# Streamed tiles and weights at many distances modulo 512 bytes

## Chip, cores and metric

One core of one Trainium2 chip runs the whole program. The metric is device time in microseconds, the median of three runs. The four inputs of attention and the weights of two feed-forward stages lie in HBM; the result goes back to HBM.

## What is computed

The reference has three stages, one behind the other, in float32 (some inputs arrive as 64-bit words, which the kernel turns into float32 itself):

```python
state = gamma * state + k_t v_t^T ; y_t = scale * q_t state     # 4 batches, 8 heads, 768 steps, 64 wide
xn = x / rms(x) * rms_g                                          # x: 3072 tokens x 512
x  = (silu(xn @ w_gate) * (xn @ w_val)) @ w_out                  # 512 -> 1536 -> 512
h  = x @ w_in ; solu = h * softmax(h) ; out = layernorm(solu) * g_ln @ w_out2   # 512 -> 1024 -> 512
```

## The kernel before

The 3072 tokens go in six blocks of 512 (`NB`), numbered 0 to 5. A block's hidden width of 1536 goes in twelve groups of 128 (`NM`). Every large product is made of three matmuls: each float32 operand is split into a high and a low part (type fp32r), and `mm3` (lines 775 to 778) adds high by high, high by low and low by high into one PSUM bank. A matmul has two operands in SBUF: the weights (`lhsT`, 128 columns, 512 bytes per partition), which a weight-load instruction brings into TensorE, and the streamed tile (`rhs`, mostly 512 columns, 2048 bytes per partition), which runs past them.

Per group `m`, `bc_block` (line 813) streams the normalised activations `xnh` and `xnl` past the gate and val weights (tiles `w`, tag `w4`, four buffers) into the banks GB and VB (`gv`), makes silu(gate) times val and its two parts `ah` and `al` (tag `r2`, eight buffers), and one group later streams these past the output weights (tag `wo`, two buffers) into four banks X0 to X3 (`cmm`, line 800). From block 1 on, these weights are loaded from a scratch copy in HBM by `w_load` (line 699), on the queue of SyncE. In block 0 the even groups use the same tiles and the odd ones the tile `CV`. Block 5 forms the gate and val products from sums of quarters (`seven_block`, matmuls on line 888, 256 streamed columns); there the four summed activations stand in tiles of the tags `rq`, `rk`, `kd` and `qd`. The last stage of a block streams `w2ih` and `w2il` past parts of x (`d_mm`, or the quarter products on line 1150, which also stream `xnh`, `xnl` and tiles of `w4` past tiles of `r2` and `x2`), transposes the result (line 1018) and streams `w2oh` and `w2ol` past the transposed parts, which are `r2` tiles (`e_mm`, line 1036). Attention of the next block is woven between these matmuls.

Addresses. The program keeps a row of fixed tiles (pool `cp`), and behind them the rotating tiles (pool `wp`), tag by tag in the order of the first request, all buffers of a tag one behind the other, each rounded up to 32 bytes per partition. `spacer` and `gap` reserve bytes that nothing uses. Nearly every tile is 2048 or 4096 bytes long, so a tag's buffers all have the same remainder of their address modulo 512. "Distance" below is the address of the streamed tile minus that of the weights loaded while it streams (those of the next matmul), modulo 512. Slices of a tile start at multiples of 512 bytes, so a distance depends on the tiles alone. The remainders of the kernel before:

| tiles | remainder |
|---|---|
| w2ih, w2il, xnh, xnl, U, w2oh, w2ol, CV, x2, r2, f4, st, w4, wo, rv, A | 448 |
| rq, rk, kd, qd | 352 |

So every product of fp32r parts has distance 0, but for the four summed tiles of block 5, which have 416.

Of the kernel before, what the change touches and what calls it, by code (L numbers as in the profile page):

```python
# [18 lines left out]
P = 128  # L19
# [23 lines left out]
def retention_moe_kernel(ctx: ExitStack, tc: tile.TileContext, qk0, q2, kt, kv, wpk, w2i, w2o,  # L43
# [3 lines left out]
    wp = ctx.enter_context(tc.tile_pool(name="wp", bufs=1))  # L47
# [13 lines left out]
    def spacer(n, name):  # L61
        cp.tile([P, n // 4], F32, tag=name, name=name)

    spacer(320, "sp0")
    QK = cp.tile([P, NCB, 2, 4, P], F32, tag="w2ih", name="QK")
    KV = cp.tile([P, NCB, 2, 512], F32, tag="w2il", name="KV")
    w2 = {}
# [8 lines left out]

    cnt = [0]

    def wt(tag, shape, dt, bufs):
        cnt[0] += 1  # L80
        return wp.tile(shape, dt, tag=tag, name=f"{tag}_{cnt[0]}", bufs=bufs)

    gaps = set()

    def gap(name, n):
        if name not in gaps:
            gaps.add(name)
            wp.tile([P, n // 4], F32, tag=name, name=name, bufs=1)

    def st():  # L90
        return wt("st", [P, 512], F32, 3)

    def f4():
        return wt("f4", [P, 2, 512], F32, 3)

    def r2():
        return wt("r2", [P, 512], F32R, 8)
# [36 lines left out]
            nc.vector.tensor_tensor(out=new, in0=new, in1=sv, op=ALU.add)  # L134

    def unit_load(gc, u):
        gap("gq", 416)
        tq = wt("rq", [P, 4, P], F32, 2)
        nc.sync.dma_start(tq, q2[gc, u])
        if u == 0:  # L140
            rawk[gc] = wt("rk", [P, 4, P], F32, 2)
            nc.sync.dma_start(rawk[gc], kt[gc])
        gap("gr", 96)
        tv = wt("rv", [P, 512], F32, 2)
        nc.sync.dma_start(tv, kv[gc, u])
        raw[gc, u] = (tq, tv)
# [701 lines left out]
    bufs = {"w4": 4, "rv": 2, "x2": 4}  # L848
# [513 lines left out]
    for i in (m0, m1, m2, m3) if SCOPE else (m1, m2, m3):  # L1362
        after.enter_context(tc.issue_after(i.ins))
    pk(3), first_decay(3), state(3), upd(3)
    unit_load(NCB, 0)
    unit_load(NCB, 1)
    unit_prep(NCB, 0)

# [116 lines left out]
```

## Time and profile before

| | |
|---|---|
| median of three runs | 980.13 us (978.42 to 980.45) |
| span of the profiled execution | 977.1 us |
| TensorE busy in it | 964.0 us, 5868 matmuls |
| VectorE, GpSimd, ScalarE busy | 504.5, 435.2, 423.0 us |
| weight loads on TensorE | 802.8 us, beside the matmuls |

The profiled execution has its span, from the first instruction to the last, as its own time; the median of the runs is 3.0 us longer (980.13 less 977.1), which holds what lies around the span. Matmuls overlap in the profile: the time that one costs is the spacing from its start to the next one's, and its listed duration is longer by a fixed part.

### The profile page before, as it was taken

What the parts mean: (1) busy time and instruction counts of PE and PEld (TensorE: products, weight loads), DVE (VectorE), ACT (ScalarE), POOL (GpSimd) and SP (SyncE); (2) the same over time, 40 slices, a digit from 0 to 9 for tenths busy, and PEclk for the clock granted to TensorE, in tenths of its full rate; (3) what the DMA queues carried; (4) which work ended last, traced back from release to release, by engine and by line L of the source; (5) the groups of instructions that cost most, each with busy time, mean ns of one, the idle gap of its engine ahead of it and who ended that gap; (6) DMA issues with size and microseconds to landing.
All of it is one profiled execution on the core that took longest, in us unless ns stands there. A gap on an engine that the chain in (4) does not pass through costs nothing.

```text
span 977.1 us, 15991 instructions
## 1 busy us (share of the span) xinstructions
PE 964.0 (99%) x5868; PEld 802.8 (82%) x5868; DVE 504.5 (52%) x996; ACT 423.0 (43%) x824; POOL 435.2 (45%) x473
## 2 busy tenths in 40 slices
PE   8999999999999999999999999999999999999998
PEld 7878787888888888888888888888888888999987
DVE  5788784662465743433574233476233366343473
ACT  4767664582345444222355122346312246321254
POOL 6976873671142494443437234438132426300022
PEclk9799999999999999999999999999999999999999
DMA  9799999887513116898833789952698954798501
GB/s 347 246 329 404 351 318 386 316 322 231 189 35 96 56 44 198 294 309 271 290 115 117 277 292 352 311 171 80 204 340 297 322 187 132 242 319 293 192 1 44
DMA packets 94990, 227.64 MB, mean 233 GB/s; under 512 B 10816, under 2 KB 36800, under 8 KB 93888
## 3 DMA queue, kind: packets, MB, share of 16 engines
q1 hardware_dynamic: 86128, 201.44, 60.3%
q10 hardware_dynamic: 8784, 25.17, 6.7%
q8 instruction: 47, 0.77, 0.3%
q14 instruction: 31, 0.25, 0.1%
HBM read 184.63 MB, written 41.94 MB: 232 GB/s over the span
## 4 chain that ended last, share of the span: by engine, by line
PE 90%; POOL 3%; DMA 2%; DVE 2%; ACT 2%; issue 1%; SPq 0%; ACTq 0%; POOLq 0%
PE X L776 11%; PE X L778 10%; PE X L777 10%; PE GB L776 7%; PE GB L778 6%; PE GB L777 6%; PE VB L776 6%; PE VB L778 6%; PE VB L777 6%; PE SB L119 3%; PE X L1150 3%; PE GB L1150 2%; PE VB L1150 2%; PE YB L119 2%; PE VB L888 2%; PE YB L888 2%
## 5 line engine op out<-in xcount | busy, mean ns | idle before, releaser
L795 DVE TENSOR_TENSOR f<-VB,f 128x512 f32<-128x512 f32 x60 | 41.4, 690 | 131.3 <-PE VB L778 117.4
L777 PE MATMUL X<-r,wo 128*128 128x512 f32 x260 | 101.7, 391 | 0.0
L778 PE MATMUL X<-r,wo 128*128 128x512 f32 x260 | 101.4, 390 | 0.0
L776 PE MATMUL X<-r,wo 128*128 128x512 f32 x260 | 99.9, 395 | 0.0
L824 ACT ACTIVATE f<-GB 128x512 f32<-128x512 f32 x60 | 35.7, 595 | 142.7 <-PE GB L778 141.9
L100 ACT CAST r<-f 128x512 fp32r<-128x512 f32 x72 | 44.5, 619 | 117.2 <-DVE f L795 99.0
L677 POOL TENSOR_TENSOR st<-st,x 128x512 int32<-128x512 int32 x52 | 70.5, 1359 | 46.5 <-DVE st L676 11.8
L776 PE MATMUL GB<-xnh,w 128*128 128x512 f32 (+1 forms) x220 | 86.5, 393 | 1.1 <-ACT xnh L100 0.8
L777 PE MATMUL GB<-xnl,w 128*128 128x512 f32 (+1 forms) x220 | 85.7, 390 | 0.2 <-DVE xnl L101 0.2
L776 PE MATMUL VB<-xnh,w 128*128 128x512 f32 (+1 forms) x220 | 85.7, 390 | 0.0
L778 PE MATMUL GB<-xnh,w 128*128 128x512 f32 (+1 forms) x220 | 85.5, 389 | 0.1
L778 PE MATMUL VB<-xnh,w 128*128 128x512 f32 (+1 forms) x220 | 85.2, 387 | 0.3 <-POOL w L101 0.3
L777 PE MATMUL VB<-xnl,w 128*128 128x512 f32 (+1 forms) x220 | 85.1, 387 | 0.0
L101 DVE TENSOR_TENSOR r<-f,r 128x512 fp32r<-128x512 f32 x72 | 60.5, 842 | 32.5 <-ACT r L100 32.0
L572 POOL TENSOR_TENSOR x<-x 128x512 f32<-128x512 f32 x24 | 31.5, 1314 | 97.4 <-DMA x<-scr 73.7
L101 POOL TENSOR_TENSOR r<-st,r 128x512 fp32r<-128x512 f32 x8 | 10.9, 1367 | 114.7 <-ACT r L100 114.7
L241 POOL TENSOR_TENSOR qd<-rq,qtab_t 128x512 f32<-128x512 f32 x14 | 18.8, 1343 | 92.2 <-DMA rq<-in_q 74.5
L776 PE MATMUL X<-w2oh,r 128*128 128x512 f32 (+1 forms) x144 | 57.3, 398 | 1.1 <-ACT f L1058 0.6
L778 PEld LDWEIGHTS X<-r,wo 128*128 128x128 f32 x260 | 48.8, 188 | 10.2
L776 PEld LDWEIGHTS X<-r,wo 128*128 128x128 f32 x260 | 48.7, 188 | 10.2 <-ACT r L100 0.2
L777 PEld LDWEIGHTS X<-r,wo 128*128 128x128 f32 x260 | 48.8, 188 | 9.9 <-issue 0.2
L778 PE MATMUL X<-w2oh,r 128*128 128x512 f32 (+1 forms) x144 | 55.6, 386 | 0.0
(452 smaller groups left out, 2489.5 us busy)
## 6 DMA issues: line engine op xcount, KB each, us to landing
w<-scr SPq DMA_DIRECT2D x96, 512.0 KB, 4.9
wo<-scr SPq DMA_DIRECT2D x59, 512.0 KB, 5.0
x<-in_wpk SPq DMA_DIRECT2D x36, 512.0 KB, 6.7
x<-scr SPq DMA_DIRECT2D x25, 512.0 KB, 5.9
sscr<-x SPq DMA_DIRECT2D x24, 512.0 KB, 7.8
scr<-CV ACTq DMA_DIRECT2D x18, 512.0 KB, 6.6
rv<-in_kv SPq DMA_DIRECT2D x24, 256.0 KB, 4.1
scr<-w ACTq DMA_DIRECT2D x12, 512.0 KB, 6.1
```

Source lines behind the costliest of these rows:

```text
L100: h = nc.scalar.copy(hi, src)
L101: (lo_eng or nc.vector).tensor_tensor(out=lo, in0=src, in1=hi.bitcast(F32), op=ALU.subtract)
L119: return lambda: nc.tensor.matmul(out, lhsT=lhsT, rhs=rhs, start=start, stop=stop)
L572: nc.gpsimd.tensor_tensor(out=w[:, 0, :], in0=w[:, 0, :], in1=w[:, 1, :], op=ALU.add)
L677: nc.gpsimd.tensor_tensor(out=ti, in0=ti, in1=lo, op=ALU.add)
L776: nc.tensor.matmul(ps, lhsT=lh, rhs=rh, start=start, stop=False)
L777: nc.tensor.matmul(ps, lhsT=lh, rhs=rl, start=False, stop=False)
L778: return nc.tensor.matmul(ps, lhsT=ll, rhs=rh, start=False, stop=stop)
L795: recent["dve"] = nc.vector.tensor_tensor(out=a, in0=GV[1], in1=silu[:, 0, :], op=ALU.mult)
L824: recent["act"] = nc.scalar.activation(s[:, 0, :], GV[0], AF.Silu)
L888: nc.tensor.matmul(ps, lhsT=x, rhs=y[:, k, :], start=start and k + i == 0, stop=k == 1 and i == 2, skip_group_check=True)
L1150: last["mm"] = nc.tensor.matmul(bank, lhsT=x[:, k, ts_], rhs=y[:, k, :], start=start and k + i == 0, stop=k == 1 and i == 2, skip_group_ch ...
```

## The change

The spacer ahead of the fixed tiles goes (320 bytes), and one gap shrinks by 384. The 704 bytes are given to three tags: each buffer of `r2` is 16 bytes longer (32 with the rounding), of `w4` 80 (96), of `wo` 8 (32), and half of the tiles of `wo`, those with an odd running number, begin 8 bytes into their buffer. No instruction is added, removed or moved, and no size of a transfer changes.

```diff
-    spacer(320, "sp0")
...
+    pads = {"r2": 16, "w4": 80, "wo": 8}
+
     def wt(tag, shape, dt, bufs):
         cnt[0] += 1
-        return wp.tile(shape, dt, tag=tag, name=f"{tag}_{cnt[0]}", bufs=bufs)
+        n = 1
+        for x in shape[1:]:
+            n *= x
+        if tag not in pads:
+            return wp.tile(shape, dt, tag=tag, name=f"{tag}_{cnt[0]}", bufs=bufs)
+        t = wp.tile([P, n + pads[tag] // 4], dt, tag=tag, name=f"{tag}_{cnt[0]}", bufs=bufs)
+        o = 2 * (cnt[0] % 2) if tag == "wo" else 0
+        t = t[:, o:o + n]
...
     def unit_load(gc, u):
-        gap("gq", 416)
+        gap("gq", 32)
```

Worked out from these sizes, the remainders become:

| tiles | before | after |
|---|---|---|
| w2ih, w2il, xnh, xnl, U, w2oh, w2ol, CV, x2 | 448 | 128 |
| r2, buffers 0 to 7 | 448 | 128, 160, 192, 224, 256, 288, 320, 352 |
| f4, st | 448 | 384 |
| w4, buffers 0 to 3 | 448 | 384, 480, 64, 160 |
| wo, buffers 0 and 1 | 448 | 256 or 264, 288 or 296 |
| rq, rk, kd, qd | 352 | 352 |
| rv, A | 448 | 448 |

## Rows read from the trace of the kernel before

**Rows 1.** The page: span, busy time by engine, granted clock and DMA by slice.
```profile
span 977.1 us, 15991 instructions
PE 964.0 (99%) x5868; PEld 802.8 (82%) x5868; DVE 504.5 (52%) x996; ACT 423.0 (43%) x824; POOL 435.2 (45%) x473
PEclk9799999999999999999999999999999999999999
DMA  9799999887513116898833789952698954798501
```

**Rows 2.** The page: chain of waits that ended last, by engine.
```profile
PE 90%; POOL 3%; DMA 2%; DVE 2%; ACT 2%; issue 1%; SPq 0%; ACTq 0%; POOLq 0%
```

**Rows 3.** Busy time by stretch: stretch, length, busy us per engine, clock, DMA share, GB/s.
```profile
165.00:760.00 595.00, 595.00 (x3639) 487.62 (x3638) 275.99 (x560) 237.11 (x473) 260.37 (x285) 1.00 0.65 219
760.00:925.00 165.00, 164.08 (x1003) 145.35 (x1002) 78.24 (x180) 58.76 (x115) 40.99 (x48) 1.00 0.71 244
```

**Rows 4.** Timeline of TensorE behind a pause: start us, duration us, operation.
```profile
302.19 0.47 PE L776 MATMUL X<-w2oh,r 128*128 128x512 f32 x1
302.50 0.39 PE L777 MATMUL X<-w2ol,r 128*128 128x512 f32 x1
...
304.58 0.39 PE L777 MATMUL X<-w2ol,r 128*128 128x512 f32 x1
...
305.49 0.39 PE L778 MATMUL X<-w2oh,r 128*128 128x512 f32 x1
```

**Rows 5.** Timeline of TensorE's weight loads in the same stretch.
```profile
304.59 0.19 PEld L778 LDWEIGHTS X<-w2oh,r 128*128 128x128 f32 x1
```

**Rows 6.** Matmuls of line 1150: duration ns min/median/max.
```profile
L1150 PE MATMUL X<-w2ih,x x32: 389/389/389, 484.1 to 943.8; 128*128 128x512 f32 x32
L1150 PE MATMUL GB<-xnl,r x24: 389/389/389, 488.2 to 935.6; 128*128 128x512 f32 x24
```

**Rows 7.** Matmuls of line 888: duration ns min/median/max.
```profile
L888 PE MATMUL SB<-xnh,w x20: 277/283/283, 821.4 to 910.2; 128*128 128x256 f32 x20
L888 PE MATMUL SB<-rq,w x18: 277/280/283, 833.9 to 910.9; 128*128 128x256 f32 x18
L888 PE MATMUL VB<-qd,A x36: 277/280/283, 843.0 to 917.2; 128*128 128x256 f32 x36
```

**Rows 8.** Groups of TensorE by line and form: count, busy us, mean ns, idle before.
```profile
L777 PE MATMUL X<-r,wo 128*128 128x512 f32 x260 | 101.7, 391 | 0.0
L776 PE MATMUL GB<-xnh,w 128*128 128x512 f32 x212 | 83.5, 394 | 0.8 <-ACT xnh L100 0.8
L776 PE MATMUL X<-w2oh,r 128*128 128x512 f32 x136 | 55.0, 404 | 1.1 <-ACT f L1058 0.6 <-ACT r L1021 0.5
L776 PE MATMUL GB<-w2oh,r 128*128 128x512 f32 x48 | 18.9, 395 | 0.0
L1150 PE MATMUL X<-w,r 128*128 128x512 f32 x48 | 12.2, 389 | 0.0
```

**Rows 9.** Matmuls of line 776 that write X from r2 and wo: duration ns min/median/max.
```profile
L776 PE MATMUL X<-r,wo x260: 387/389/501, 49.3 to 922.9; 128*128 128x512 f32 x130
```

**Rows 10.** Transposes of line 1018: duration ns min/median/max.
```profile
L1018 PE MATMUL X<-ident,f x136: 270/272/327, 280.3 to 965.4; 128*128 128x128 f32 x136
```

**Rows 11.** DMA issues: KB each, median us from issue to landing.
```profile
wo<-scr SPq DMA_DIRECT2D x59, 512.0 KB, 5.0
```

More of the change, by code (lines that the diff above doesn't have):

```diff
@@ L77, in retention_moe_kernel @@
     cnt = [0]
+    pads = {"r2": 16, "w4": 80, "wo": 8}
     def wt(tag, shape, dt, bufs):
         cnt[0] += 1
-        return wp.tile(shape, dt, tag=tag, name=f"{tag}_{cnt[0]}", bufs=bufs)
+        n = 1
[6 more added lines that the diff above has]
+        t = t[:, o:o + n]
+        if len(shape) == 3:
+            t = t.rearrange("p (a x) -> p a x", a=shape[1])
+        if len(shape) == 4:
+            t = t.rearrange("p (a b x) -> p a b x", a=shape[1], b=shape[2])
+        return t
     gaps = set()
```

## The prediction

> **What bounds the kernel now.** I read the page first. TensorE is busy 99% of the span and every other compute engine about half of it [rows 1]. The chain of waits that ended last lies to 90% on TensorE [rows 2], and in the long middle (165 to 760 us) the engine is busy for all of the 595 us, in block 5 for 164.08 of 165 us [rows 3]. The granted clock stays at its upper level, 2.4 GHz, in both stretches [rows 3]. So the time is the sum of the spacings of TensorE's matmuls, and only what changes a spacing changes the time. In the timeline the reader is to look at starts, not at durations: four spacings from 304.58 to 305.49 us take 0.91 us, 227 ns each, where 512 columns at 2.4 GHz would be 213 ns [rows 4]. The listed duration is 389 ns there, so a spacing is the duration less 162 ns, and durations in the other views can be compared in single ns. The next matmul's weights are loaded at the same time: the load for the matmul of 304.81 starts at 304.59, 0.01 us behind the matmul of 304.58 [rows 4, 5]. So two streams read SBUF side by side, and their distance modulo 512 is what the edit alters.
>
> Two more things are to be seen. First, at distance 0 the matmul repeats itself to the ns: 32 and 24 in a group with minimum, median and maximum all 389 [rows 6]. Second, behind a pause it doesn't: the nine spacings from 302.50 to 304.58 take 2.08 us, 231.1 ns each, 4 ns more than the settled ones [rows 4]. It takes several matmuls to find the pace of 227. I read this as a repeating state that the equal spacing of equal pairs makes possible; that it needs one constant distance is my inference, no row shows it for 512 columns.
>
> **The change part by part.**
>
> The instructions. None is added, moved or removed; engines other than TensorE have the same tile sizes, and their remainders stay multiples of 32 bytes, but for half of the output weights. I cost ScalarE, VectorE and GpSimd at nothing: they are idle about half of the span, TensorE covers them, and if that cover went, one of their operations late by tens of ns would be lost in spacings of the same size.
>
> How many matmuls get another distance. Gate and val: six groups of 212 (two banks, three matmuls), 1272. Output products: three of 260, 780. Last products: three of 136 and three of 48, 552. Quarter products with an r2 or w4 tile: 48, and by the same view 144 more, 192 [rows 8]. Sum 2796. A few keep distance 0 (r2's buffer 0 against the fixed tiles, some pairs at the seams of two groups); by the remainders about 2650 change. Gate and val get 256, 160, 64 and 480, one value for the twelve matmuls of a tile. The output products get 18 values that differ between neighbours, since the high and low parts lie in different buffers. The last products get 480 down to 288 in steps of 32, again different between neighbours.
>
> What another distance costs. For 512 columns no row has one, so I bound it. The nearest rows are those of 256 columns in block 5: at distance 0 the median is 283 ns, at 416 it is 280, and the extremes are 277 and 283 on both sides [rows 7]. So the low end is -3 ns per matmul, 2650 x -3 ns = -8.0 us; with the minimum (-6 ns) -15.9 us. On the other side stands the stretch in which 512 columns have not settled: +4 ns, 2650 x 4 ns = +10.6 us. The upper end of the sum I take as twice that, +8 ns, +21 us, should a worse pace repeat. I take the unsettled stretch as the value, because it is the row with the same column count and the same tiles, but only where the distance changes from matmul to matmul: output, last and quarter products, 1524 less some 150 that keep distance 0, 1374 x 4 ns = +5.5 us. Gate and val have a constant distance for twelve matmuls, so I let them settle there, and count a fresh start for each of 1272 / 12 = 106 tiles; a start costs up to 9 x 4 = 36 ns [rows 4], half of that taken, since some starts will fall near the pace: 106 x 18 ns = +1.9 us.
>
> Block 5 itself. Its products on line 888 with xnh and xnl stand at 0 against w4 and rv and leave it; at -3 ns for some 180 of them -0.5 us. The summed tiles have 416 or other values before and after, taken as no change.
>
> Transposes. Lines of f4 move from distance 256 to 0. No row prices it, and the nearest is block 5's 3 ns between two distances [rows 7, 10]: 160 x 3 ns, up to 0.5 us either way, taken as +0.2.
>
> The 8 bytes. Half of the output weights start 8 bytes off. Their load lands in 5.0 us [rows 11], and a group of 36 matmuls takes 36 x 0.227 = 8.2 us, with two buffers, so a load that got slower by half would still be in time; past that it would end a wait. Cost taken: nothing. As weights, the 0.19 us load [rows 5] lies beneath a spacing of 0.227.
>
> Sum: 5.5 + 1.9 - 0.5 + 0.2 = +7.1 us. The profiled 977.1 us become 984.2; with the 3.0 us by which the median exceeds the span, 987.2.
>
> A rule that speaks against all of this: the Trainium skill, "SBUF — State Buffer", section "Who interferes with whom", gives TensorE two independent read ports, one for the streamed operand and one for the weights, and says that it never waits on anyone. By that rule a distance can't matter. Rows 7 differ by 3 ns between distances with the same columns, and the trace so far doesn't bear the rule out fully; it is rival A's ground.
>
> **The rivals.**
>
> A, nothing happens. The extra 14 ns per matmul come from the switch of weights and not from addresses. For it: spacing less columns is about the same for 512 and 256 columns at distance 0 (389 - 162 - 213 = 14; 283 - 162 - 107 = 14) [rows 6, 7]. Against it: rows 7. Time 980.1, chance 0.15.
>
> B, faster. Distance 0 is the bad one because both streams start in the same place, and every other distance gives what 416 gives in block 5: -3 ns each, -8.0 us, 972.1; with the minimum of the rows, 964. For it: the median of 280 against 283 [rows 7]. Against it: at 256 columns a weight load of 0.19 us is nearly as long as the matmul and both may wait for each other; at 512 columns it is not, and there unsettled matmuls are slower than settled ones, not faster. Decides from an average spacing under 227. Chance 0.25.
>
> C, slower still: a worse pace repeats in all 2650, +8 ns, 1001. Nothing but groups' means above 389, as 394 and 404 [rows 8], speaks for it, and these hold the matmuls at pauses. Chance 0.07.
>
> D, the output weights come late: the loads into 8-byte remainders take longer than a group (8.2 us against 5.0 [rows 11]), and TensorE waits in each of some 50 groups. From 1 us late per group +50 us. DMA is below full share in the middle (0.65 and 0.71 [rows 3]), which speaks against it. Chance 0.03.
>
> **How the numbers follow.** The forecast itself, 981.5 to 996 around 987.2, has 0.50. Slower by over 0.2% (2 us, about what a measurement of this kernel can tell from no change) is the forecast with C and D, 0.60; within 0.2% is A, 0.15; faster is B, 0.25. The range has to take in B's 972 and stop short of D and the far end of C: 971 to 1000; the forecast's own range is 981.5 to 996.
>
> **What would show it.** Right: TensorE's count stays 5868, its idle time stays near 13 us, and the listed mean durations rise, for the output products from 391 to about 395, with the median no longer the minimum plus 2 [rows 8, 9]; gate and val rise less, and their median stays at 389. Line 1150's groups with x alone stay at 389/389/389. Wrong: durations below 389 as the rule for a whole group (B), all medians at 389 as before (A), or a new wait of TensorE for wo (D).

## The result: 13.9 us slower, and the profile after

The changed kernel takes 993.54 us (median of four runs, 989.81 to 994.85) against 979.62 us of the kernel before on the same chip: ratio 1.0135, 95% interval 1.0114 to 1.0155 (the quotient of the two medians is 1.0142). That is +13.9 us, with 11.2 to 15.2 by the interval. The prediction said 987.2 us in a range of 971 to 1000: the sign is right, the size (+7.1 us in its sum) is half of what was measured.

First the page of the changed kernel, the lines that answer to [rows 1, 2].

```profile
span 991.8 us, 15991 instructions
PE 978.5 (99%) x5868; PEld 806.2 (81%) x5868; DVE 506.2 (51%) x996; ACT 422.8 (43%) x824; POOL 436.1 (44%) x473
PEclk8899999999999999999999999999999999999999
...
PE 90%; POOL 3%; DMA 3%; DVE 2%; ACT 1%; issue 1%; SPq 1%; ACTq 0%; DVEq 0%; POOLq 0%
```

The span grew by 14.7 us (991.8 less 977.1) and TensorE's busy time by 14.5 (978.5 less 964.0), with the same 5868 matmuls. Its idle time is 13.3 us after 13.1. So no wait was added, the chain is as before, and the matmuls themselves stand further apart. The table by stretch says the same (columns as in [rows 3]):

```profile
165.00:760.00 595.00, 595.00 (x3573) 480.94 (x3573) 271.23 (x551) 236.19 (x471) 261.76 (x285) 1.00 0.63 216
760.00:925.00 165.00, 164.08 (x1001) 142.86 (x1000) 79.36 (x180) 57.27 (x113) 42.19 (x49) 1.00 0.72 246
```

TensorE is busy for all of the 595 us at granted clock 1.00 and starts 66 matmuls fewer in them (3573 for 3639). Now the timeline of TensorE at the place of [rows 4], behind the same pause:

```profile
308.76 0.48 PE L789 MATMUL X<-w2oh,r 128*128 128x512 f32 x1
309.07 0.39 PE L790 MATMUL X<-w2ol,r 128*128 128x512 f32 x1
...
311.86 0.40 PE L790 MATMUL X<-w2ol,r 128*128 128x512 f32 x1
312.09 0.39 PE L791 MATMUL X<-w2oh,r 128*128 128x512 f32 x1
```

From 309.07 to 312.09 lie thirteen spacings, 232.3 ns each. In the kernel before the first nine took 231.1 ns each and the next ones 227. Here the pace of 227 is not found, as the prediction had taken it for these products. The groups by line (lines are 13 further down than before; columns as in [rows 8]):

```profile
L790 PE MATMUL X<-r,wo 128*128 128x512 f32 x260 | 102.6, 394 | 0.0
...
L789 PE MATMUL GB<-xnh,w 128*128 128x512 f32 x212 | 84.2, 397 | 0.9 <-ACT xnh L113 0.9
...
L789 PE MATMUL X<-w2oh,r 128*128 128x512 f32 x136 | 55.4, 407 | 1.0 <-ACT f L1071 0.6 <-ACT r L1034 0.5
...
L1163 PE MATMUL X<-w,r 128*128 128x512 f32 x48 | 12.5, 395 | 0.0
```

The means rise by 3 ns for the output and last products, and by 3 for gate, which the prediction had let settle; the quarter products with w4 rise by 6. The rows below give minimum, median and maximum of single groups; they answer to [rows 9, 6, 7, 10], and the second fence is gate, in the kernel before and in the changed one (it holds 8 matmuls of 256 columns beside the 212).

```profile
L789 PE MATMUL X<-r,wo x260: 387/394/506, 52.1 to 937.1; 128*128 128x512 f32 x130
```

```profile
L776 PE MATMUL GB<-xnh,w x220: 283/389/579, 34.6 to 780.2; 128*128 128x512 f32 x106, 128*128 128x256 f32 x4
...
L789 PE MATMUL GB<-xnh,w x220: 278/394/580, 36.3 to 793.5; 128*128 128x512 f32 x106, 128*128 128x256 f32 x4
```

```profile
L1163 PE MATMUL X<-w,r x48: 389/394/399, 495.7 to 957.0; 128*128 128x512 f32 x48
...
L1163 PE MATMUL X<-w2ih,x x32: 387/389/397, 493.0 to 958.4; 128*128 128x512 f32 x32
```

```profile
L901 PE MATMUL SB<-xnh,w x20: 276/280/283, 835.4 to 924.4; 128*128 128x256 f32 x20
L901 PE MATMUL SB<-rq,w x18: 274/281/287, 848.0 to 925.1; 128*128 128x256 f32 x18
```

```profile
L1031 PE MATMUL X<-ident,f x136: 270/272/328, 286.7 to 980.2; 128*128 128x128 f32 x136
```

The output products' median went from 389 to 394: it is the rule that moved, not the edge. So did gate's, where the prediction's sign was a median that stays at 389. On line 1163 the pair w2ih against x2, which keeps its distance of 0, still has the median 389, though its extremes are now 387 and 397, while its neighbour with w4 and r2 has the median 394. Of 256 columns, xnh past w fell from 283 to 280. The transposes are unchanged. The load of the output weights lands later than in [rows 11], and no wait of TensorE names it:

```profile
wo<-scr SPq DMA_DIRECT2D x59, 512.0 KB, 5.6
```

The last transpose row holds a ruler that the experiments need. From the first transpose to the last, the kernel before takes 685.1 us (965.4 less 280.3 [rows 10]) and the changed one 693.5: +8.4 us in that stretch. The other 6.3 us (14.7 less 8.4) lie before it. Nearly half of them are still the same matter, in blocks 0 and 1: if the two traces' matmuls are matched one by one in the order of their starts, the changed kernel is 3.6 us behind at 111 us and 6.4 at the first transpose (286.7 less 280.3), and from 111 to 280 us both have the granted clock at 1.00. The changed kernel and then the kernel before, in that stretch:

```profile
111.00:280.00 169.00, 167.85 (x843) 135.68 (x842) 93.59 (x142) 87.43 (x154) 86.04 (x70) 1.00 0.80 283
```

```profile
111.00:280.00 169.00, 167.98 (x874) 137.78 (x875) 95.39 (x152) 89.41 (x159) 85.84 (x71) 1.00 0.79 278
```

So 11.2 of the 14.7 us come behind 111 us, at the upper level of the clock. The 3.6 us before that lie where the granted clock still moves. The next rows are the stretch from 12 to 16 us, in the changed kernel and then in the kernel before, and one group of block 0 whose distance is 0 in both, after and then before.

```profile
12.00:16.00 4.00, 4.00 (x47) 3.55 (x45) 1.67 (x5) 1.81 (x6) 2.47 (x4) 0.58 1.03 408
```

```profile
12.00:16.00 4.00, 3.46 (x47) 3.27 (x48) 2.74 (x7) 2.26 (x7) 3.85 (x5) 1.00 1.04 404
```

```profile
L789 PE MATMUL GB<-xnh,CV 128*128 128x512 f32 x24 | 10.2, 426 | 0.0
```

```profile
L776 PE MATMUL GB<-xnh,CV 128*128 128x512 f32 x24 | 9.7, 405 | 0.0
```

The granted clock is 0.58 there, so mostly the lower level of 1.2 GHz, where the kernel before has the upper one of 2.4 GHz throughout (1.00); TensorE itself was busy for all of the 4 us, and for 8.62 of the 12 us ahead of them. From 60 to 100 us the clock is 0.96 against 1.00, and a group whose distance did not change got 21 ns dearer in the mean. The kernel before has such a stretch too, at another place: over the first 111 us its clock is 0.95, that of the changed kernel 0.92. Stretches at the lower level lie in the first 180 us of every profile of the whole kernel below, at places that differ. So a single profile is compared from the first transpose on, which leaves out what blocks 0 and 1 cost ahead of it, and whole times by their medians.

### The profile page after: what moved, and what is told of

It reads as the page before. It is cut to its first block, busy times and chain, and to the rows that moved or that the text cites. A ratio compares the mean times of both kernels' runs of the same rounds, so it can differ in the third digit from the quotient of the medians.

```text
span 991.8 us, 15991 instructions
## 1 busy us (share of the span) xinstructions
PE 978.5 (99%) x5868; PEld 806.2 (81%) x5868; DVE 506.2 (51%) x996; ACT 422.8 (43%) x824; POOL 436.1 (44%) x473
## 4 chain that ended last, share of the span: by engine, by line
PE 90%; POOL 3%; DMA 3%; DVE 2%; ACT 1%; issue 1%; SPq 1%; ACTq 0%; DVEq 0%; POOLq 0%
PE X L789 11%; PE X L791 10%; PE X L790 10%; PE GB L789 7%; PE GB L791 7%; PE GB L790 7%; PE VB L789 6%; PE VB L791 6%; PE VB L790 6%; PE X L1163 3%; PE SB L132 3%; PE GB L1163 2%; PE VB L1163 2%; PE YB L132 2%; PE VB L901 2%; PE YB L901 2%
## 5 line engine op out<-in xcount | busy, mean ns | idle before, releaser
L790 PE MATMUL X<-r,wo 128*128 128x512 f32 x260 | 102.6, 394 | 0.0
L791 PE MATMUL X<-r,wo 128*128 128x512 f32 x260 | 102.4, 394 | 0.0
L789 PE MATMUL X<-r,wo 128*128 128x512 f32 x260 | 101.1, 400 | 0.0
L789 PE MATMUL VB<-xnh,w 128*128 128x512 f32 (+1 forms) x220 | 87.2, 396 | 0.0
L791 PE MATMUL VB<-xnh,w 128*128 128x512 f32 (+1 forms) x220 | 86.6, 394 | 0.0
```

The costliest lines, as they stand in the source:

```text
L789: nc.tensor.matmul(ps, lhsT=lh, rhs=rh, start=start, stop=False)
L790: nc.tensor.matmul(ps, lhsT=lh, rhs=rl, start=False, stop=False)
L791: return nc.tensor.matmul(ps, lhsT=ll, rhs=rh, start=False, stop=stop)
```

## The experiments

The theory that they test: every distance between the streamed tile and the weights of the next matmul has a pace of its own; a few distances have the pace of 227 ns for 512 columns, the others have slower ones. Rivals: a constant distance settles wherever it lies and only the alternation of distances costs (the prediction's sizing of gate and val); the absolute remainder counts; the traffic of the other engines does it. Nine kernels were run. Each ratio is against runs of the kernel before on the same chip, whose medians were 979.62, 979.81 or 979.86 us.

**All remainders moved together.** The kernel before without its first spacer: every tile moves by the same 320 bytes, all distances stay.

```diff
-    spacer(320, "sp0")
```

> The kernel before without its first spacer: every tile's remainder modulo 512 is 320 lower (the fixed and rotating tiles 128, the four summed tiles 32) and every distance between a streamed tile and its weights is as before. Theory 1 (the distance alone sets the pace of the matmuls): 979.6 us, within 2 us, and 389 ns medians. Theory 2 (changing the distance from matmul to matmul is what costs, any constant one is as good): the same 979.6. Rival 3 (the absolute remainder sets the pace, 448 being a good one): towards the changed kernel, 988 to 994.

Measured: 980.48 us, ratio 1.0005, interval 0.9989 to 1.0021, and the groups keep their means:

```profile
L776 PE MATMUL X<-r,wo 128*128 128x512 f32 x260 | 101.7, 391 | 0.0
```

The absolute remainder is out.

**One constant distance, 256 or 160.** The kernel before with one gap ahead of the tiles of w4, so that gate, val and output products all stand at a single other distance.

```diff
+        if tag == "w4":
+            gap("gw", 256)      # the other kernel: 352
...
-        gap("gq", 416)
+        gap("gq", 160)          # the other kernel: 64
```

> The kernel before with a gap of 256 bytes ahead of the gate/val and output weights (the later gap is 256 smaller): every gate/val and output product has the constant distance 256 instead of 0. Theory 1, from the changed kernel's stretches at 256, which settle at spacings of 226 and 227 ns: 979.6 within 2 us. Theory 2: the same. If 0 is the only good distance: some 2050 matmuls x 4 to 6 ns, 988 to 992.

> As the kernel with distance 256, but with a gap of 352: constant distance 160 for about 2050 matmuls of gate/val and output products. Theory 1, from the changed kernel's stretches at 160 (spacings walk 231 to 238, mean 234 ns): 2050 x 7 ns = +14.4, about 994 us (991 to 996). Theory 2: any constant distance settles, 979.6 within 2 us.

Measured at 256: 979.71 us, ratio 0.9991, interval 0.9974 to 1.0008. At 160: 995.29 us, ratio 1.0162, interval 1.0114 to 1.0211. Two groups and the transposes at 256:

```profile
L779 PE MATMUL X<-r,wo 128*128 128x512 f32 x260 | 101.7, 391 | 0.0
...
L778 PE MATMUL GB<-xnh,w 128*128 128x512 f32 x212 | 83.5, 394 | 0.4 <-ACT xnh L102 0.4
```

```profile
L1020 PE MATMUL X<-ident,f x136: 270/272/328, 281.5 to 967.0; 128*128 128x128 f32 x136
```

and at 160:

```profile
L779 PE MATMUL X<-r,wo 128*128 128x512 f32 x260 | 103.3, 397 | 0.0
...
L778 PE MATMUL GB<-xnh,w 128*128 128x512 f32 x212 | 84.8, 400 | 0.4 <-ACT xnh L102 0.4
```

```profile
L1020 PE MATMUL X<-ident,f x136: 270/272/328, 285.0 to 980.2; 128*128 128x128 f32 x136
```

Nothing alternates in these products in either kernel. At 256 the means are those of [rows 8] to the ns, at 160 they are 6 ns higher in both groups. Between first and last transpose 256 takes 685.5 us (before: 685.1) and 160 takes 695.2, +10.1 us. A distance does not get the pace of 227 ns by being constant. This takes the ground from the prediction's term for gate and val, and from the alternation as the only cause.

**The pace of each distance by itself.** A program of matmuls alone, in chains of 40 to 48, each chain with one streamed tile (saa, sab, ... each 32 bytes further modulo 512) past four weight slices of one tile in turn; a second set begins 16 bytes further, a third alternates two tiles, a fourth lies 8 bytes off. It was run once.

```diff
+    for i in range(16):
+        chain(48, 512, [at(i, 512)])
+    for i in range(16):
+        chain(48, 512, [at(i, 512, 4)])
+    for i in range(16):
+        chain(40, 256, [at(i, 256)])
...
+    for i, o in ((0, 2), (0, 6), (8, 2), (15, 6)):
+        chain(48, 512, [at(i, 512, o)])
```

> Not the reference's work: chains of 48 matmuls of one streamed slice with one pair of weight tiles and nothing else running; 32 chains of 512 columns at distances 0 to 496 in steps of 16 bytes, the same with 256 columns in chains of 40, then five chains that alternate between two distances (0 and 256, 0 and 32, 64 and 320, 0 and 96, 64 and 128) and four at 8-byte distances. Theory 1: 512 columns settle to 227 ns at 0 and 256, to 229 at 64, 234 at 160, and stay between 225 and 236 elsewhere; 0 with 256 in turn is 227 as well. Theory 2: 227 ns at every constant distance, and 231 or more where two alternate. If other engines' traffic makes the difference: one spacing everywhere.

One row for each of some chains follows, from narrow stretches of the trace; durations are ns, minimum, median and maximum. In order: distances 0, 160 and 256 with 512 columns; 0, 160, 192 and 448 with 256 columns; 8 bytes with 512 columns.

```profile
L74 PE MATMUL X<-saa,w x49: 389/389/389, 16.3 to 27.2; 128*128 128x512 f32 x49
...
L74 PE MATMUL X<-saf,w x48: 388/397/400, 72.0 to 83.0; 128*128 128x512 f32 x48
...
L74 PE MATMUL X<-sai,w x47: 389/389/395, 105.7 to 116.1; 128*128 128x512 f32 x47
...
L74 PE MATMUL X<-saa,w x40: 278/283/283, 373.3 to 377.9; 128*128 128x256 f32 x40
...
L74 PE MATMUL X<-saf,w x39: 277/280/282, 397.0 to 401.5; 128*128 128x256 f32 x39
...
L74 PE MATMUL X<-sag,w x39: 276/276/279, 401.7 to 406.0; 128*128 128x256 f32 x39
...
L74 PE MATMUL X<-sao,w x40: 276/276/279, 439.5 to 443.9; 128*128 128x256 f32 x40
...
L74 PE MATMUL X<-saa,w x48: 392/396/402, 579.1 to 590.1; 128*128 128x512 f32 x48
```

Only 0 and 256 have the median 389 of [rows 6]; at 160 the median is 397 over a whole chain. The spacings, worked out from the starts in the trace, each a mean from the chain's 15th start to its last, ns:

| distance | 512 columns | 256 columns |
|---|---|---|
| 0, 256 | 226.7 | 120.0 |
| 32 | 233.3 | 117.8 |
| 64, 320 | 228.9 | 117.8 |
| 96 | 233.3 | 120.0 |
| 128 | 233.5 | 118.7 |
| 160, 416 | 234.1 | 117.3 |
| 192, 448 | 233.4 | 113.3 |
| 224 | 233.4 | 118.2 |
| 8, 24, 264, 504 | 233.3 | not run |
| 0 and 32 in turn | 231.7 | not run |
| 0 and 256 in turn | 226.7 | not run |
| 64 and 320 in turn | 228.9 | not run |
| 0 and 96 in turn | 230.0 | not run |
| 64 and 128 in turn | 233.5 | not run |

The chains that begin 16 bytes further lie between 231.1 and 234.8 ns with 512 columns; with 256 columns two of their distances modulo 256, 16 and 112, have 113.3 as well, and the others 117.2 to 119.9. A distance d and d + 256 give the same pace (to 0.1 ns in the table, to 0.3 in the chains 16 bytes further), so what counts is the distance modulo 256, not 512. Two tiles 256 bytes apart cost nothing in turn. VectorE does nothing in this program, and ScalarE and GpSimd next to nothing behind its first slices, and the paces of the full kernel are there: the other engines' traffic is not the cause.

**Gate and val alone, and everything but them.** The first kernel lengthens only the buffers of w4; the second is the changed kernel with the lengthening of w4 taken away. The gaps are set so that all other distances stay as in the kernel before, or after. The cut is against the changed kernel.

```diff
-    pads = {"r2": 16, "w4": 80, "wo": 8}
+    pads = {"w4": 80}           # the second kernel: {"r2": 16, "wo": 8}
```

> The kernel before with only the gate and val weights spread: w4's four buffers 96 bytes apart, every other product of the kernel before at its old distance (r2, wo and the fixed tiles alike, the summed tiles 416 against A). Gate and val then stand at 0, 416, 320 and 224, which modulo 256 are the distances of the change. Pace theory (each distance but 0 and 256 has a slower pace of its own that never settles to 227): about 1180 matmuls of 512 columns; by the spacings of the changed kernel, xnh past w4 764 x (231.6 - 227.6) + xnl past w4 416 x (230.9 - 227.6) = +4.4 us, 984.0. The prediction's own sizing (a constant distance settles, only a fresh start per tile costs): +1.9 us and -0.5 on line 888, 981.0. Rows of TensorE: the group xnh past w, 512 columns, rises from a mean of 394 to about 398, the group r2 past wo stays at 391.

> The changed kernel with the longer w4 buffers taken away, so that gate and val stand at the constant distance 256 and line 888 at 256; r2 and wo keep their spread buffers and the 8 bytes. Pace theory: gate and val go back to 227, about 4.4 us less than the changed kernel, 989.1, or +9.5 us over the kernel before, all of it in the products with r2 and wo. The prediction's own sizing: the terms left are the output, last and quarter products, 5.5 us over before, 985.1. Rows of TensorE: r2 past wo stays at a mean of 394, xnh past w goes back from 398 to 394.

Measured: w4 alone 986.55 us, ratio 1.0068, interval 1.0049 to 1.0087; without w4 990.33 us, ratio 1.0102, interval 1.0083 to 1.0121. The kernel with w4 alone:

```profile
L792 PE MATMUL X<-r,wo 128*128 128x512 f32 x260 | 101.8, 391 | 0.0
...
L793 PE MATMUL VB<-xnh,w 128*128 128x512 f32 x212 | 84.1, 397 | 0.2 <-POOL w L116 0.2
```

```profile
L1033 PE MATMUL X<-ident,f x136: 270/272/327, 285.2 to 973.8; 128*128 128x128 f32 x136
```

Three starts of its timeline show the pace of single tiles. Between the first two stream the twelve matmuls of a gate tile at distance 0, 227.5 ns each; between the last two the twelve of the val tile behind it, at distance 224, 233.3 ns each:

```profile
177.64 0.39 PE L791 MATMUL GB<-xnh,w 128*128 128x512 f32 x1
...
180.37 0.39 PE L791 MATMUL VB<-xnh,w 128*128 128x512 f32 x1
...
183.17 0.39 PE L791 MATMUL X<-r,wo 128*128 128x512 f32 x1
```

The kernel without it:

```profile
L790 PE MATMUL X<-r,wo 128*128 128x512 f32 x260 | 102.6, 395 | 0.0
...
L791 PE MATMUL VB<-xnh,w 128*128 128x512 f32 x212 | 82.8, 391 | 0.3 <-POOL w L114 0.3
```

```profile
L1031 PE MATMUL X<-ident,f x136: 270/272/327, 283.6 to 974.6; 128*128 128x128 f32 x136
```

Each kernel slows the groups whose distance it moves (in the first, val's 397 also holds matmuls of up to 632 ns at the lower clock, from 158 to 165 us). In the second, gate rises too, though it stands at the constant 256: by 1, 3 and 1 ns on its three lines (val by none), 5 ns x 212 = 1.1 us. Its gate tiles come behind the spread output products and open with up to nine spacings of 224 to 240 ns before they take 227, and most val tiles behind them have 227 from the start: that is the fresh start that the prediction had priced, for about half of its tiles. Between the transposes w4 alone costs 3.5 us (688.6 less 685.1) and the rest 5.9 (691.0 less 685.1), 9.4 in sum where the whole change costs 8.4. Gate and val are no small term: +6.7 us by the medians (4.8 to 8.5 by the interval), where the prediction's sizing gave +1.4. It misses; the theory's +4.4 lies just under the interval, and this kernel's trace has 4.6 us behind 170 us, where the clock is at its upper level.

**Faster distances in block 5.** The sweep has a better pace for 256 columns, 113.3 ns at 192 and 448. The first kernel moves the four summed tiles 32 bytes, from 416 to 448. The second also lets block 5 keep xnh and xnl 64 bytes earlier in longer buffers, so that all of its products on that line stand at 192 modulo 256.

```diff
-        gap("gq", 416)
+        gap("gq", 448)
...
-            xs[key] = xnh[:, k, ts_], xnl[:, k, ts_]
+            xs[key] = xnh7[:, k, ts_], xnl7[:, k, ts_]   # the second kernel
```

> The kernel before with block 5's summed tiles (rq, rk, kd, qd) 32 bytes further, so that their distance to A and the weights of w4 becomes 448 in place of 416; everything else stays. Pace theory: in the sweep, 256 streamed columns cost 117.3 ns at 416 and 113.3 at 448, and about 286 matmuls stream these tiles; 286 x 4 to 4.8 ns gives -1.1 to -1.4 us, 978.2 to 978.5. Rival (inside the kernel these 256-column matmuls are bounded by the weight load beside them, not by the distance): no change, 979.6. Rows of TensorE: the groups of rq and qd on line 888 fall from a median of 280 to about 276.

> As the kernel with the summed tiles at 448, and in block 5 the activations xnh and xnl 64 bytes earlier in their buffers as well, so that every product of line 888 streams at distance 192 modulo 256; all products of 512 columns stay at 0 or 256. Pace theory, by the sweep: some 216 more matmuls of 256 columns from 120 to 113.3 ns, -1.4 us, beside -0.85 us that the 448 gave from the start of block 5 on in its trace: about -2.3 us behind the first 180 us, 977.4. If in the kernel only half of it comes, as for the summed tiles (115.6 in place of 113.3): -1.7 us, 978.0. Rival (the 256-column pace is given by the weight load of every matmul, and xnh has a floor at 120): -0.85 us, 978.8. Rows: xnh past w on line 888 falls from a median of 283 to 276 or 277.

Measured: 979.83 us, ratio 0.9994 (0.9978 to 1.0010), and 979.39 us, ratio 0.9996 (0.9983 to 1.0009). Neither can be told from the kernel before. The line of the summed tiles in the first,

```profile
L888 PE MATMUL SB<-xnh,w x20: 277/282/283, 824.9 to 913.0; 128*128 128x256 f32 x20
...
L888 PE MATMUL SB<-rq,w x18: 276/279/284, 837.5 to 913.7; 128*128 128x256 f32 x18
```

```profile
L1018 PE MATMUL X<-ident,f x136: 270/272/327, 283.9 to 968.1; 128*128 128x128 f32 x136
```

and in the second:

```profile
L892 PE MATMUL SB<-xnh,w x20: 276/281/281, 823.5 to 911.9; 128*128 128x256 f32 x20
...
L892 PE MATMUL SB<-rq,w x18: 281/281/281, 836.0 to 912.6; 128*128 128x256 f32 x18
```

In the first the stretch between the transposes is 684.2 us, 0.9 shorter than before, with the whole difference in block 5: that is a little less than the 1.1 to 1.4 that the theory gave, and too small for the medians to show. In the second xnh's median fell from 283 to 281, not to 276, and rq's went up from 280 to 281, though all stand at 192 or 448. Its profile also has a wait of 1.5 us for VectorE at 361 us that the others lack. The sweep's 113.3 ns did not come back there; why one kernel reaches 276 in places and the other does not stays open. No version that beats the kernel before was found.

**Eight bytes.** The kernel before with every output weight tile 8 bytes into a buffer of 4352 bytes, so that r2 past wo stands at the constant distance 248.

```diff
+        if tag == "wo":
+            t = wp.tile([P, 1088], dt, tag=tag, name=f"{tag}_{cnt[0]}", bufs=bufs)[:, 2:1026]
```

> The kernel before with every output weight tile 8 bytes into its buffer (buffers 4352 bytes long, so that nothing else moves modulo 256): r2 past wo then stands at the constant distance 248 instead of 0, for about 694 matmuls of 512 columns. Pace theory with a grain of 8 bytes: the sweep's 233.3 ns against 227.6, +4.0 us, 983.8, and r2 past wo rises from a mean of 391 to about 396. Rival 1 (distances matter only in steps of 32 bytes): no change, 979.7, mean 391. Rival 2 (a start that is no multiple of 32 bytes slows the load of these tiles): its landing rises from 5.0 us to the 5.6 of the changed kernel; by the pace theory alone it stays at 5.0.

Measured: 982.20 us, ratio 1.0033, interval 1.0019 to 1.0047.

```profile
L781 PE MATMUL X<-r,wo 128*128 128x512 f32 x260 | 102.5, 394 | 0.0
```

The output products rose by 3 ns, so 8 bytes are a distance like any other. The spacing is 230.8 ns here and 233.4 in the sweep at the same distance (504, which is 248 modulo 256): the sweep gives the order, not the size to the ns. The landing of the output weights is 5.4 us after 5.0, but it is 5.8 in the kernel with w4 alone, which has no 8-byte start, and 5.2 in the one without w4, which has it. So the landing moves from kernel to kernel by more than that, and rival 2 is not shown.

## Why the prediction was right in sign and half in size

**What bounds it.** Right: only spacings of TensorE changed, at equal count and equal idle time.

**Output, last and quarter products, +5.5 us (1374 x 4 ns).** Right in size. By the means before and after, the three output groups rose by 3, 4 and 5 ns (391, 390, 395 to 394, 394, 400; 12 x 260 = 3.1 us), the last products by 11 x 136 + 8 x 48 = 1.9 us, the quarter products with r2 by 0.9 us: 5.9 us. The reason was half right. That the matmuls do not come to 227 ns is in the timeline; that it is the change from one distance to the next that keeps them from it is not, since 160 alone, held constant, costs as much.

**Gate and val, +1.9 us.** This is the step that failed: "Gate and val have a constant distance for twelve matmuls, so I let them settle there". They don't: 64, 160 and 480 have their own paces, and only 256, one of the four buffers, has 227. By the six means (394, 393, 391, 390, 390, 390 before; 397, 398, 395, 394, 394, 394 after) the term is 24 ns x 212 = +5.1 us, and the run with w4 alone has it by itself: 233.3 ns throughout a val tile at a constant distance. The prediction said that its assumption had no row; it should have put the unsettled 4 ns on all 2650 matmuls, +10.6 us, which it named only as a bound. With the other terms as they were that gives 990.4 (977.1 + 10.6 - 0.5 + 0.2 + 3.0).

**Block 5, -0.5 us.** Right in kind: xnh's median fell from 283 to 280.

**Transposes, +0.2.** Nothing: 272 before and after.

**The 8 bytes, nothing.** Right for the loads, which no matmul waited for. As a distance the 8 bytes do cost, and the output products' term already counted them.

**The sum behind 111 us.** With the spacings matched one by one, the 11.2 us there are: output, last and quarter products 5.8 (the prediction's 5.5), gate and val 5.1 (its 1.9), matmuls of 256 columns -0.4 (its -0.5), and 0.7 in small groups that it did not count. So all but 1 us of what its sum lacks there is the one term.

**What was not in the sum.** The 3.6 us before 111 us, where the changed kernel's profile has the lower granted clock for longer (0.92 against 0.95). Block 0's products with xnh and xnl past CV, whose distance did not change, are part of them: the six groups' means rose by 83 ns in sum, x 24 = 2 us. Whether the change has a part in that stays open: the kernel at 448, which moves no product of 512 columns, comes to its first transpose 3.6 us later than the kernel before (283.9 less 280.3) as well. And the 3.0 us between span and median were too much: the changed kernel's profiled run took 993.56 us in all, 1.8 more than its span.

**The rivals.** A (nothing happens) and B (every other distance is better) are out for 512 columns; the sweep has no distance below 226.7 ns. For 256 columns B has a true part, 113.3 for 120.0, but block 5 is too small for it. C (a worse pace repeats in all) is what the constant 160 does, and it was the nearer picture of gate and val. D never arose. The rule of the Trainium skill, "SBUF — State Buffer", section "Who interferes with whom", that TensorE's two read ports are independent and it never waits on anyone, is not borne out here: the same matmul has a median of 389 ns at distance 256 and 397 at 160, with no other engine at work. What in the chip makes the pace depend on the distance, no run here shows.

## What to carry to other kernels

Where TensorE is busy all the time, compare the durations of one form in single ns: where one group has a median of 389 and another, with the same form at the same clock, 394, the place of its two operands is a cause to look at. For 512 columns keep the streamed tile and the next weights a multiple of 256 bytes apart, across all buffers of a tag, and count padding inside a buffer as a change of that distance. And where a price has no row of its own, put the nearest row on everything that changes, and do not exempt a part by an assumption that no row shows.

## What the runs showed that was not expected

- The pace depends on the distance modulo 256, not 512: 160 and 416, 192 and 448, 64 and 320 agree to 0.1 ns in the sweep.
- 512 columns and 256 columns want different distances: 226.7 ns only at 0 and 256 for the one; 113.3 ns at 192 and 448, and at 16 and 112 modulo 256, for the other, where 0 is among the slowest with 120.0. In the whole kernel the second was not reached in full.
- A stretch of block 0 or 1 at a lower granted clock (0.58 from 12 to 16 us here) moves a single profile by as much as a small change does: 3.6 us at the first transpose in the kernel at 448.
